# Attention with a top-1 mixture of experts: order of the weight loads, layout of the second weights, and columns of the first product in steps of two

## The chip, the cores and the metric

One core of a Trainium2 chip runs the whole program. The metric is device time in microseconds of one execution; three executions of the kernel before are listed, and one more was recorded with a profile. Engines are called PE (TensorE), PEld (its weight loads), DVE (VectorE), ACT (ScalarE), POOL (GpSimd) and SP (SyncE, which issues most transfers).

## The reference

Block-causal attention over 8 batches of 8 heads, 576 positions of 64 elements, then a mixture of experts over the 4608 tokens of 512 elements, all in float32:

```python
scores = q @ k.T / 8, masked to block_i >= block_j (blocks of 64), softmax, @ v
x = attention output as (4608, 512)
logits = x @ w_gate                       # (4608, 8)
expert = argmax(logits); gate = softmax(logits)[expert]
for e in range(8):
    tok = tokens of expert e, at most capacity (80) of them, those of largest gate
    h = relu(x[tok] @ w1[e])              # w1[e]: (512, 1024)
    out[tok] = gate[tok] * (h @ w2[e])    # w2[e]: (1024, 512)
all other rows of out are 0
```

Each of the sixteen weight matrices is 2 MiB.

## The kernel before, in words

**Attention.** 32 pairs of heads run as a software pipeline whose order is written out by hand: the loop at line 895 goes over turns `i`, and each turn issues the steps of a table (`FIRST`, `SHARED`, `TURN`, `LAST`) for the pairs around `i`. In a turn the pair `i+5` is loaded (`load`, line 613, 72 KB per transfer, read in runs of 128 bytes; SP issues most of them, POOL the second head's K from pair 5 on), the pair `i+2` is transposed on DVE (`prep`, line 639), the scores of pair `i+1` are made on PE (lines 663, 680, 689), and the probabilities of pair `i` are turned and multiplied with the values (lines 744, 770, 775, 776). Line 680 runs once per pair near a turn's start. The `ld` tiles have four buffers.

**Early weights.** The first three matrices of the list `w1[0], w2[0], w1[1], w2[1], ...` (`FW0 = 3`) are loaded during attention by POOL, in pieces of 128 rows (line 352: 512 KB for `w1`, 256 KB for `w2`), one piece in each turn with `i >= 2 and i % 3` (line 914).

**Selection.** After the last pair the tokens' gates are ranked (lines 978 to 1090), which ends with the row numbers `gi`. POOL then gathers the rows of experts 0, 1 and 2 (line 1101, `fetch`), 80 rows of 2080 bytes each; the other gathers follow one per expert.

**Later weights.** They are issued by SP in order (line 362, `piece`; each behind the one before on SP). Before the selection `half()` loads the first half of `w2[1]` (line 951). Its other half waits for the landing of the second gather (`HOLD = 1`, lines 1020 and 1199). The next loads wait, in turn, for the landing of the load or gather that stands in `behind` (lines 1200 to 1203):

```python
other_half(fetches[HOLD])
behind = [loaded.ins, fetches[HOLD]]
for _ in range(FWA + FWC + FWB - 1):
    weights(1, behind.pop(0))
    behind.append(loaded.ins)
```

so at most two are under way. From `w2[4]` on there is one `weights(1)` in the expert loop after the first product and one after the second (lines 1363 and 1372); those wait for a free buffer, of which there are nine.

**Experts.** For each expert PE makes the first product (`first`, line 1284, through `blocks`, line 1217: 128 pairs of a weight load of 64 columns of `w1` and a matmul over 80 tokens, at line 1240; the first half of expert 0 at line 1227), ACT applies the relu into `hT`, and PE makes the second product (`second`, line 1303, matmuls at line 1325 with `hT` as stationary and `w2` as moving operand). `divide` (line 1211, DVE) scales the gathered rows, `prepare` (line 1254) transposes them, and `scatter` (line 1340) writes the result rows. In expert 0 a check of the selection runs beside it (`finish_`): DVE makes `chk` at line 1162 and PE sums it at line 1166, between the two halves of the first product.

The rows of `w2` lie on the partitions as `(a p)`: row `128 a + p` on partition `p`, so each partition takes runs of 512 elements, 2 KB. `w1` lies in the same way with runs of 1024 elements, 4 KB.

Of the kernel before, what the change touches and what calls it, by code (L numbers as in the profile page):

```python
# [7 lines left out]
F32 = mybir.dt.float32  # L8
# [10 lines left out]
P = 128  # L19
# [169 lines left out]
def tile_attn_moe(ctx, tc, q, k, v, w_gate, w1, w2, capacity, out, xs=None, dbg=None):  # L189
    nc = tc.nc  # L190
# [152 lines left out]
    def loads(n, after=None):  # L343

        nonlocal nw, loaded
        for _ in range(n):
            src, e = wlist[nw]
            w_ = wpools[nw % len(wpools)].tile([P, KP * F], F32, name="w")
            nw += 1
            wt_[src is w2, e] = w_ = w_.rearrange("p (a f) -> p a f", f=src.shape[2])  # L350
            if nw <= FW0:
                yield from (nc.gpsimd.dma_start(w_[:, a], src[e][a * P:(a + 1) * P]) for a in range(w_.shape[1]))
                continue
            piece(w_, src[e], 0, w_.shape[1], after)

    def piece(w_, src, a0, a1, after=None):

        nonlocal loaded
        with ExitStack() as order:
            if loaded is not None:  # L360
                order.enter_context(tc.issue_after(loaded.ins))
            loaded = nc.sync.dma_start(w_[:, a0:a1], src[a0 * P:a1 * P].rearrange("(a p) f -> p a f", p=P))
        if after is not None:
            tc.add_manual_dep(loaded.ins, after.name, mybir.DependencyInfo(
                mybir.DependencyClass.Sync, mybir.DependencyReason.DATA))

    def half():

        nonlocal nw
        src, e = wlist[nw]  # L370
        w_ = wpools[nw % len(wpools)].tile([P, KP * F], F32, name="w")
        nw += 1
        wt_[src is w2, e] = w_ = w_.rearrange("p (a f) -> p a f", f=src.shape[2])
        na = w_.shape[1]
        piece(w_, src[e], 0, na // 2)
        return lambda after: piece(w_, src[e], na // 2, na, after)

    Pt = [{u: pb.tile([P, 2, w], F32, name=f"P{u}_{i}") for u, w in WIDE.items()} for i in range(2)]  # L380

# [510 lines left out]
    with tc.manual_schedule():  # L892
        warm(WARM[0], banks("g")[0])
        early = loads(FW0)
        for i in range(-LEAD, n):
            held.clear()
            if i == -1:
                nc.sync.dma_start(ci, capacity.bitcast(U32).partition_broadcast(P))
                for h in range(2):
                    nc.sync.dma_start(wgd[h * D:(h + 1) * D, :, h * E:(h + 1) * E], wg_v[h])  # L900

            for _ in range(min(5, nz - kept - cleared) if i >= n - 5 else 0):
                clear(cleared, nc.sync)
                cleared += 1
            if i == 1 - LEAD:
                nc.scalar.activation(early_exp, ramp[:, 2, 0:1], AF.Exp)
                constants()
            if i == -1:
                constants2()
            if i == 5:  # L910
                nc.gpsimd.tensor_copy(cf, ci)
            if i == 7:
                constants3()
            if i >= 2 and i % 3:
                next(early, None)
            shared = i > 1 and (i < NP or i % NP == 0)
            for d, what, *args in FIRST if i == -1 else AHEAD if i == -2 else LAST if i == n - 1 else SHARED if shared else TURN:
                if what in slots_:
                    slots_[what]()
                elif 0 <= i + d < n and not (what == "flip" and n - NP <= i + d < n - 2):  # L920
                    getattr(pairs[i + d], what)(*args)
            if n - NP <= i + valued < n - 2:
                pairs[i + valued].flip()
            if i >= flipped and (i - flipped) % NP == NP - 1 and i - flipped < n - 1:
                enqueue(batches[(i - flipped) // NP])
        for _ in early:
            pass
        while not turns:
            t()
        bt = batches[B - 1]  # L930
        pairs[n - 2].flip()
        for _ in recips[0]:
            pass
        bt.store_sums()
        pairs[n - 1].take("V00", "a")
        bt.flip(NP - 1, 0, 8)
        pairs[n - 1].take("V01", "a")
        pairs[n - 1].take("V1", "v")
        att.close()
        fwa = late.enter_context(tc.tile_pool(name="fwa", bufs=FWA, **right, **tw))  # L940
        wpools += [fwa] * FWA
        bt.logits2(LAST_BANKS)
        bt.logits_by_token(NP - 1)
        bt_, mark = turns.pop(0)
        bt_.turn2(banks("av")[0])
        mark()
        for _ in bt.products(range(NP - 1)):
            pass
        bt.flip(NP - 1, 8, S // 32)
        bt.store_x()  # L950
        other_half = half()
        for _ in (*bt.products((NP - 1,)), *bt.shift()):
            pass
        bt.expo()
        nc.gpsimd.tensor_copy(seen[0:1], dl[0:1, 0, 0:1])
        found, weighed = bt.first_of(), bt.weight()
        for g_ in (found, found, found, weighed, found, weighed):
            next(g_)
        bt.turn_gated()
        bt.turn2(banks("L")[0])  # L960
        while small:
            t()
        for _ in bt.placed():
            pass
# [52 lines left out]
        for h in range(2):  # L1017
            vec.max_index(cidx[:, h], cand16[:, h], Wf[:, h * HW:(h + 1) * HW])

    HOLD = 1  # L1020
    pen = sel.tile([P, 2, NH], F32, name="pen")
    pool.tensor_scalar(pen, key, scalar1=0.0, scalar2=8192.0, op0=ALU.is_lt, op1=ALU.mult)
    pool.tensor_tensor(pen, pen, iota_c[:, 0:NH].unsqueeze(1).broadcast_to([P, 2, NH]), op=ALU.add)
# [172 lines left out]
    wpools += [fwc] * FWC + [fwb] * FWB  # L1196

    assert cleared == nz or ov is None
    other_half(fetches[HOLD])
    behind = [loaded.ins, fetches[HOLD]]  # L1200
    for _ in range(FWA + FWC + FWB - 1):
        weights(1, behind.pop(0))
        behind.append(loaded.ins)

# [9 lines left out]

    def blocks(dst, w_, x_, n, nb, after=None, pieces=None):
        if pieces is not None:
            for a in range(n):
                pieces(a, after)  # L1220
                for b in range(nb):
                    for c in range(2):
                        col = (2 * b + c) * 64
                        with ExitStack() as order:
                            if after is not None:
                                order.enter_context(tc.issue_after(after.ins))
                            after = nc.tensor.matmul(dst(b)[64 * c:64 * (c + 1)], lhsT=w_[:, a, col:col + 64],
                                                     rhs=x_[a], start=(a == 0 and b == 0),
                                                     stop=(a == n - 1 and b == nb - 1))
                yield after  # L1230
            return
        for b in range(nb):
            for a in range(n):
                for c in range(2):
                    col = (2 * b + c) * 64
                    with ExitStack() as order:
                        if after is not None:
                            order.enter_context(tc.issue_after(after.ins))
                            after = None
                        last = nc.tensor.matmul(dst(b)[64 * c:64 * (c + 1)], lhsT=w_[:, a, col:col + 64],  # L1240
                                                rhs=x_[a], start=(a == 0), stop=(a == n - 1))
                    yield last

# [330 lines left out]
```

## Time and profile before

| | |
|---|---|
| three executions | 385.63, 386.33, 386.37 us, median 386.33 |
| profiled execution | 387.1 us, of which the span of its instructions is 385.3 |
| granted TensorE clock | 0.997 |
| PE, DVE, ACT, POOL busy | 367.5, 286.0, 287.5, 183.7 us |
| transferred | 84.43 MB, mean 219 GB/s |

Attention takes the first 276 us or so, the selection until about 288, the experts until 378.8, and the last scatter and the end of the program the rest. Stretches are read by busy time per engine; DMA share is the mean busy share of 16 transfer engines and can pass 1.

### The profile page before, as it was taken

The numbers are of one execution on the slowest core, as the hardware profiler recorded it, in microseconds if no ns is written. First come the engines' busy times: TensorE is split into PE (matmuls) and PEld (weight loads), VectorE is DVE, ScalarE is ACT, GpSimd is POOL, SyncE is SP. The second block draws the span as 40 slices with busy tenths as digits, with TensorE's granted clock in tenths as the row PEclk, the third lists the DMA queues.
The fourth block names the chain that finished last, engine by engine and source line by source line (L and its number), as shares of the span: only waits on it lengthen the run. The fifth ranks groups of instructions, "written<-read, shape, count | busy, mean of one in ns | idle before, by whom it ended". The sixth has DMA issues, their size and how long they took to land. (4 is left out here: it accounts for less than half of the span.)

```text
span 385.3 us, 15173 instructions
## 1 busy us (share of the span) xinstructions
PE 367.5 (95%) x5973; PEld 248.4 (64%) x5973; DVE 286.0 (74%) x804; ACT 287.5 (75%) x880; POOL 183.7 (48%) x377
## 2 busy tenths in 40 slices
PE   5899899999999999999999999999999999999983
PEld 3566567666766666676676676666668555555652
DVE  5889799999999999999999999999986210101001
ACT  1799799999999999999999999999521333332221
POOL 6246376665976766786587664430132121110000
PEclk9999999999999999999999999999999999999998
DMA  9969999999999999999999999999795899999950
GB/s 125 154 120 187 133 184 173 154 231 132 164 215 151 162 202 181 155 176 196 177 174 245 145 182 191 279 393 407 157 212 167 278 384 374 384 391 398 399 211 26
DMA packets 169937, 84.43 MB, mean 219 GB/s; under 512 B 132590, under 2 KB 151886, under 8 KB 169857
## 3 DMA queue, kind: packets, MB, share of 16 engines
q1 hardware_dynamic: 158368, 61.80, 76.3%
q0 software_dynamic: 9120, 21.27, 24.2%
q8 instruction: 49, 0.80, 1.0%
q10 hardware_dynamic: 2368, 0.30, 0.6%
q14 instruction: 32, 0.25, 0.3%
HBM read 63.21 MB, written 20.33 MB: 217 GB/s over the span
## 5 line engine op out<-in xcount | busy, mean ns | idle before, releaser
L710 ACT ACTIVATE P<-bank,negm 128x512 f32<-128x512 f32 (+3 forms) x320 | 157.6, 549 | 10.6 <-DVE negm L699 5.9
L663 PE MATMUL bank<-T,qt 64*128 64x320 f32 (+3 forms) x512 | 98.8, 494 | 1.4 <-DVE PT L792 1.3
L770 PE MATMUL bank<-PT,vn 128*64 128x64 f32 (+3 forms) x1288 | 88.9, 292 | 0.0
L699 DVE TENSOR_REDUCE negm<-bank 128x1 f32<-128x320 f32 (+2 forms) x192 | 83.4, 474 | 5.6 <-PE bank L689 5.4
L792 ACT COPY PT<-bank 128x512 f32<-128x512 f32 x149 | 77.2, 636 | 3.8 <-PE bank L744 3.3
L770 PEld LDWEIGHTS bank<-PT,vn 128*64 128x64 f32 x1288 | 57.1, 137 | 26.7 <-ACT PT L792 3.4
L646 POOL TENSOR_SCALAR qt<-T 128x128 f32<-128x128 f32 (+2 forms) x96 | 31.2, 344 | 88.4 <-DVE T L639 88.4
L744 PEld LDWEIGHTS bank<-ident,P 64*128 64x128 f32 (+1 forms) x1600 | 58.0, 137 | 11.8 <-issue 6.6
L663 PEld LDWEIGHTS bank<-T,qt 64*128 64x128 f32 x512 | 47.9, 187 | 26.8 <-ACT PT L792 15.2
L744 PE MATMUL bank<-ident,P 64*128 64x64 f32 (+1 forms) x1600 | 63.5, 225 | 1.3 <-ACT P L710 0.6
L710 ACT ACTIVATION_READ_ACCUMULATOR P<-bank,negm 128x1 f32 x256 | 61.7, 241 | 0.0
L699 DVE TENSOR_REDUCE raw<-bank 128x1 f32<-128x64 f32 (+1 forms) x128 | 51.8, 444 | 2.3 <-PE bank L663 2.0
L639 DVE STREAM_TRANSPOSE T<-ld 128x576 f32<-128x576 f32 x64 | 49.1, 768 | 5.7 <-DMA ld<-in_k_dram 4.0
L632 POOL DMA_DIRECT2D vn<-in_v_dram x58 | 45.8, 792 | 1.2 <-issue 0.7
L1325 PE MATMUL av<-w,hT 128*32 128x512 f32 (+2 forms) x320 | 39.0, 553 | 0.0
L624 POOL DMA_DIRECT2D ld<-in_k_dram x54 | 37.3, 695 | 2.7 <-DMA ld<-in_q_dram 2.7
L1334 DVE SCALAR_TENSOR_TENSOR y<-av,comb,yt 80x512 f32<-80x512 f32 (+1 forms) x8 | 5.6, 696 | 43.0 <-ACT yt L1332 42.9
L1240 PE MATMUL ps<-xsT,w 128*64 128x80 f32 x896 | 33.1, 234 | 0.3 <-issue 0.3
L1240 PEld LDWEIGHTS ps<-xsT,w 128*64 128x64 f32 x896 | 31.9, 137 | 1.9 <-PE av L1325 1.0
L1340 POOL DMA_INDIRECT out_dram<-y,si x8 | 7.5, 936 | 53.6 <-DVE y L1334 41.3
L1332 ACT ACTIVATE yt<-ps,gfar 32x512 f32<-32x512 f32 (+2 forms) x18 | 11.4, 635 | 26.1 <-PE ps L1325 26.0
L792 DVE COPY PT<-bank 128x512 f32<-128x512 f32 x43 | 29.3, 683 | 0.3
(202 smaller groups left out, 423.9 us busy)
## 6 DMA issues: line engine op xcount, KB each, us to landing
w<-in_moe_w_dram SPq DMA_DIRECT2D x12, 2048.0 KB, 17.6
xs<-Y SPq DMA_DIRECT2D x32, 288.0 KB, 5.5
out_dram<-zero SPq DMA_DIRECT2D x18, 512.0 KB, 7.6
ld<-in_q_dram SPq DMA_DIRECT2D x126, 72.0 KB, 5.5
vn<-in_v_dram POOLq DMA_DIRECT2D x58, 128.0 KB, 5.1
ld<-in_k_dram SPq DMA_DIRECT2D x72, 72.0 KB, 5.3
w<-in_moe_w_dram POOLq DMA_DIRECT2D x8, 512.0 KB, 6.6
ld<-in_k_dram POOLq DMA_DIRECT2D x54, 72.0 KB, 6.4
```

Of the source, the lines that this page charges most:

```text
L624: eng.dma_start(self.nat[x][r], (q, k)[x][b, h0 + h, :, 32 * i:32 * i + 32] .rearrange("(g r) d -> r g d", r=32))
L632: eng.dma_start(self.vn[:, h], v[b, h0 + h, 0:512].rearrange("(j p) d -> p j d", p=P))
L639: nc.vector.transpose(t, self.nat[x].rearrange("p g d -> p (g d)"))
L646: nc.gpsimd.tensor_scalar(qb[:, to], tb[:, of], scalar1=SCALE, scalar2=1.0, op0=ALU.mult, op1=ALU.mult)
L663: nc.tensor.matmul(s[h][:, c:c + n], lhsT=q_[:, P * t - BLK:P * t + BLK], rhs=k_[:, 0:n], start=(c == 0 and g != "2"), stop=(g == "1"))
L699: nc.vector.tensor_reduce(to[:, b, h:h + 1], self.s[g][h][:, c:c + n], axis=AX.X, op=ALU.max, negate=True)
L710: nc.scalar.activation(Pt[self.i % 2][u][:, h, c1:c1 + n], self.s[g][h][:, c:c + n], AF.Exp, bias=self.negm[:, t, h:h + 1], scale=1.0, acc ...
L744: nc.tensor.transpose(pt[c][0:cols.stop - cols.start, n_ * BLK:(n_ + 1) * BLK], row[u][r, h, cols], ident[r, r])
L770: nc.tensor.matmul(a4[r] if c0 is None else av[r, BLK * c0:BLK * (c0 + b1 - b0)], lhsT=self.vn[:, h, j, :], rhs=self.PT[:, h, row, b0:b1]. ...
L792: (nc.scalar.copy if (eng or TAKE[x]) == "a" else nc.vector.tensor_copy)(*self.out.pop(x))
L1240: last = nc.tensor.matmul(dst(b)[64 * c:64 * (c + 1)], lhsT=w_[:, a, col:col + 64], rhs=x_[a], start=(a == 0), stop=(a == n - 1))
L1325: last = nc.tensor.matmul(to[col:col + s1 - s0, c0:c1], lhsT=hT[:, a, s0:s1], rhs=w_[:, a, c0:c1], start=(a == ends[0]), stop=(a == ends[1 ...
```

## The change

The half load goes; `w2[1]` is loaded whole, and it and the next load both wait for the landing of the first gather. Early pieces go out in turns with `i >= 6 and i % 3`, and those of `w2[0]` are four of 512 KB. In every `w2` a partition gets two neighbouring rows per group of 256 (row `256 g + 2 p + j` on partition `p`), which is a run of 4 KB. So that the hidden units of `hT` lie in the same order, the first product's blocks take columns of `w1` in steps of two (`pairs_of`).

```diff
             if nw <= FW0:
+                if src is w2:
+                    to, of = in_twos(w_, src[e])
+                    yield from (nc.gpsimd.dma_start(to[:, g], of[:, g]) for g in range(to.shape[1]))
+                    continue
                 yield from (nc.gpsimd.dma_start(w_[:, a], src[e][a * P:(a + 1) * P]) for a in range(w_.shape[1]))
                 continue
-            piece(w_, src[e], 0, w_.shape[1], after)
+            load_w(w_, src is w2, src[e], after)
+
+    def in_twos(w_, src):
+        return w_.rearrange("p (g j) f -> p g (j f)", j=2), src.rearrange("(g p j) f -> p g (j f)", p=P, j=2)
...
-            loaded = nc.sync.dma_start(w_[:, a0:a1], src[a0 * P:a1 * P].rearrange("(a p) f -> p a f", p=P))
+            loaded = nc.sync.dma_start(*(in_twos(w_, src) if twos else (w_, src.rearrange("(a p) f -> p a f", p=P))))
...
-            if i >= 2 and i % 3:
+            if i >= 6 and i % 3:
                 next(early, None)
...
-        other_half = half()
...
-    HOLD = 1
+    HOLD = 0
...
-    other_half(fetches[HOLD])
-    behind = [loaded.ins, fetches[HOLD]]
-    for _ in range(FWA + FWC + FWB - 1):
+    behind = [fetches[HOLD], fetches[HOLD]]
+    for _ in range(FWA + FWC + FWB):
         weights(1, behind.pop(0))
         behind.append(loaded.ins)
...
+    def pairs_of(b, c):
+        at = 256 * (b // 2) + 128 * c + b % 2
+        return slice(at, at + 127, 2)
...
-                        col = (2 * b + c) * 64
+                        cols = pairs_of(b, c)
...
-                            after = nc.tensor.matmul(dst(b)[64 * c:64 * (c + 1)], lhsT=w_[:, a, col:col + 64],
+                            after = nc.tensor.matmul(dst(b)[64 * c:64 * (c + 1)], lhsT=w_[:, a, cols],
...
-                        last = nc.tensor.matmul(dst(b)[64 * c:64 * (c + 1)], lhsT=w_[:, a, col:col + 64],
+                        last = nc.tensor.matmul(dst(b)[64 * c:64 * (c + 1)], lhsT=w_[:, a, cols],
```

## Rows read from the trace of the kernel before

**Rows 1.** The page: busy time, share and instructions; PE's busy tenths in 40 slices.

```profile
PE 367.5 (95%) x5973; PEld 248.4 (64%) x5973; DVE 286.0 (74%) x804; ACT 287.5 (75%) x880; POOL 183.7 (48%) x377
...
PE   5899899999999999999999999999999999999983
```

**Rows 2.** Stretches of attention: busy us (x instructions) per engine, clock, DMA share, GB/s.

```profile
32.00:42.00 10.00, 9.81 (x159) 7.09 (x159) 7.03 (x17) 8.92 (x27) 6.50 (x12) 1.00 1.19 188
50.00:60.00 10.00, 10.00 (x182) 6.93 (x179) 9.71 (x26) 9.62 (x30) 7.35 (x14) 1.00 1.21 185
180.00:230.00 50.00, 50.00 (x851) 34.48 (x848) 48.42 (x127) 49.11 (x159) 34.68 (x71) 1.00 1.14 184
250.00:270.00 20.00, 19.96 (x341) 13.72 (x335) 18.49 (x52) 19.02 (x61) 4.11 (x9) 1.00 1.03 398
```

**Rows 3.** Timeline of PE, line 680: start us, us, what, once per pair.

```profile
22.32 0.30 PE L680 MATMUL bank<-T,qt 64*64 64x64 f32 x8
...
30.09 0.33 PE L680 MATMUL bank<-T,qt 64*64 64x64 f32 x8
...
39.13 0.24 PE L680 MATMUL bank<-T,qt 64*64 64x64 f32 x1
...
48.19 0.43 PE L680 MATMUL bank<-T,qt 64*64 64x64 f32 x8
...
56.05 0.30 PE L680 MATMUL bank<-T,qt 64*64 64x64 f32 x8
```

**Rows 4.** Timelines of DVE and PE around 42 us, idle time before in brackets.

```profile
41.42 0.78 DVE L639 STREAM_TRANSPOSE T<-ld 128x576 f32<-128x576 f32 x1 [2.78 <-DMA ld<-in_k_dram]
...
43.36 1.99 PE L663 MATMUL bank<-T,qt 64*128 64x512 f32 x12 [1.28 <-DVE PT L792]
```

**Rows 5.** Timelines of POOL and SP: early pieces, and a K load.

```profile
31.95 0.59 POOL L352 DMA_DIRECT2D w<-in_moe_w_dram  x1
...
58.18 0.59 POOL L352 DMA_DIRECT2D w<-in_moe_w_dram  x1
...
32.05 1.09 SPq L624 DMA_DIRECT2D ld<-in_k_dram  x2
```

**Rows 6.** Stretches of the expert stage, columns as in rows 2.

```profile
299.00:301.00 2.00, 2.00 (x21) 0.60 (x24) 0.00 (x0) 0.44 (x1) 0.96 (x1) 1.00 0.32 31
301.00:371.40 70.40, 70.05 (x1240) 43.07 (x1233) 10.31 (x33) 22.56 (x40) 10.46 (x11) 1.00 1.03 383
```

**Rows 7.** Timeline of PE: the last expert's first product and the start of its second.

```profile
367.00 4.65 PE L1240 MATMUL ps<-xsT,w 128*64 128x80 f32 x128
373.38 0.52 PE L1325 MATMUL pm<-w,hT 128*32 128x384 f32 x3 [1.73 <-SPq L1386]
```

**Rows 8.** Timeline of SP: the first weight loads behind the gathers.

```profile
293.28 0.39 SPq L362 DMA_DIRECT2D w<-in_moe_w_dram  x1
...
299.33 0.92 SPq L362 DMA_DIRECT2D w<-in_moe_w_dram  x2
```

**Rows 9.** Timelines of DVE, PE and POOL at the first expert; the gathers' median landing.

```profile
291.94 0.29 DVE L1211 TENSOR_TENSOR xn<-xg 80x128 f32<-80x128 f32 x1 [0.50 <-DMA xg<-xs,gi]
...
296.71 2.29 PE L1240 MATMUL ps<-x,w 128*64 128x80 f32 x60
...
291.43 0.97 POOL L1101 DMA_INDIRECT xg<-xs,gi  x1 [0.31 <-issue]
...
295.05 0.27 DVE L1211 TENSOR_TENSOR xn<-xg 80x128 f32<-80x128 f32 x1
...
xg<-xs,gi POOLq DMA_INDIRECT x8, 6.8
...
296.61 0.17 PE L1166 MATMUL pm<-chk,ones 128*128 128x10 bf16 x1
```

**Rows 10.** Groups by line and form: busy us, mean ns of one, idle before.

```profile
L1240 PEld LDWEIGHTS ps<-xsT,w 128*64 128x64 f32 x896 | 31.9, 137 | 1.9 <-PE av L1325 1.0 <-issue 0.4
L663 PEld LDWEIGHTS bank<-T,qt 64*128 64x128 f32 x512 | 47.9, 187 | 26.8 <-ACT PT L792 15.2 <-issue 5.1 <-DVE PT L792 1.8
...
L1240 PE MATMUL ps<-xsT,w 128*64 128x80 f32 x896 | 33.1, 234 | 0.3 <-issue 0.3
```

More of the change, by code (lines that the diff above doesn't have):

```diff
@@ L351, in loads, with load_w @@
             if nw <= FW0:
+                if src is w2:
+                    to, of = in_twos(w_, src[e])
+                    yield from (nc.gpsimd.dma_start(to[:, g], of[:, g]) for g in range(to.shape[1]))
+                    continue
                 yield from (nc.gpsimd.dma_start(w_[:, a], src[e][a * P:(a + 1) * P]) for a in range(w_.shape[1]))
                 continue
-            piece(w_, src[e], 0, w_.shape[1], after)
-    def piece(w_, src, a0, a1, after=None):
+            load_w(w_, src is w2, src[e], after)
+    def in_twos(w_, src):
+        return w_.rearrange("p (g j) f -> p g (j f)", j=2), src.rearrange("(g p j) f -> p g (j f)", p=P, j=2)
+    def load_w(w_, twos, src, after=None):
         nonlocal loaded
@@ L365, in piece @@
                 mybir.DependencyClass.Sync, mybir.DependencyReason.DATA))
[L367 to L376, printed above, removed]
     Pt = [{u: pb.tile([P, 2, w], F32, name=f"P{u}_{i}") for u, w in WIDE.items()} for i in range(2)]
@@ L1234, in blocks @@
                 for c in range(2):
-                    col = (2 * b + c) * 64
+                    cols = pairs_of(b, c)
                     with ExitStack() as order:
```

## The prediction

> **What bounds the kernel now.** I read the page first, then stretches, then single waits. PE is busy for 95% of the span [rows 1], so only a few microseconds can be won, where PE stands still. The busy tenths show where: besides the first slices and the selection, slice 5 (38.5 to 48 us) has an 8, and the end falls off [rows 1].
>
> At the first place, 32 to 42 us, DVE is busy 7.03 of 10 us and the DMA share is 1.19; later, as in 180 to 230 us, PE runs without a gap [rows 2]. The starts of line 680, one per pair of heads, give the beat: 7.77 us (22.32 to 30.09), then 9.04 and 9.06 (to 39.13 and 48.19), then 7.86 [rows 3]. Two turns are too long by 1.2 each against their neighbours, 2.5 us together. What they wait for: DVE stands 2.78 us for the K tile of a later pair, after which PE idles 1.28 us [rows 4]. Just ahead are the first early piece of the weights, issued by POOL at 31.95, and the K loads of that pair, which SP issues only at 32.05 [rows 5] and which land at 41.4, 9.4 us later.
>
> At the second place, the expert stage, DMA and PE run level. From 301 to 371.4 us PE is busy for 70.05 of 70.4 us and DMA moves 383 GB/s at a share of 1.03 [rows 6]. But the last first product ends at 367.00 + 4.65 = 371.65 and the last second product begins at 373.38, after 1.73 us of idle that is put to SP, that is to the last weights [rows 7]; their data had ended at about 371.4, 2.0 us before. So the weights are late by less than two microseconds, at the very end. The lateness was made at the start: SP waits until 293.28, loads a half, and issues the next loads only at 299.33, when that has landed [rows 8]. In 299 to 301 us DMA moves 31 GB/s [rows 6].
>
> **The change part by part.**
>
> *Early pieces from turn 6.* The three pieces up to 58.18 us [rows 5] go away there; twelve of 512 KB come at the places of turns 7 to 23, in place of sixteen. POOL saves four issues of 0.59 us [rows 5]; it is busy 48% [rows 1], so that is 0. Of the three, the latter two cost nothing now (PE is busy 10.00 of 10 us between 50 and 60 [rows 2]). The first is 0.524 MB. At 398 GB/s, which DMA reaches in another stretch [rows 2], it holds the engines for 1.3 us, where they are never free [rows 2]. What is queued behind it, the K tile above all, can land 1.3 us earlier. Lower bound 0 (the K tile is late through SP's own backlog); upper bound the whole excess of 2.5. I take 1.3, since the K tile's queue shortens by just that. Turns 13 to 17 get 512 KB where 256 KB stood; pieces of 512 KB go out between 180 and 230 us too, with PE at 50.00 of 50 [rows 2], so 0; should that cover go, 1.3 per piece at worst.
>
> *No half load, weights behind the first gather.* The half lay under the selection and nothing waited for it; the gathers wait for the selection's indices and not for it, so its removal gains nothing there, and 1.05 MB more must come later. In return SP starts when the first gather lands, about 291.9 (DVE begins on it at 291.94 [rows 9]), with two whole loads at once. Data follow an issue by about 1.7 us (299.33 [rows 8], full rate from 301 [rows 6]), so they move from 293.6 on. Loads go in order with two outstanding: the third is issued when the first has landed, while the second still moves, so I see no gap. The sum: 70.4 us at 383 GB/s are 26.96 MB, of which 25.17 are twelve loads. After the change it is 26.96 + 2.10 (the load of `w2[1]`) + 0.17 (the third gather) = 29.2 MB, 76.3 us at the same rate; from 293.6 that ends at 369.9 instead of 371.4, 1.5 us earlier. With the same 2.0 us from the end of data to PE the second product starts at 371.9, and 0.25 of the idle 1.73 stays. Buffers don't hold this up: the first to be taken again, that of `w1[0]`, is read for the last time by the first product that begins at 296.71 [rows 9]. Bounds: 0, and 1.73, where PE becomes the limit.
>
> *Two rows per partition in `w2`.* The same bytes in runs of 4 KB, like those of `w1`, in place of 2 KB. The 383 GB/s [rows 6] are a mean over both; the stretch in which the output is cleared, mostly by 4 KB runs, gives 398 [rows 2], 4% more with other traffic in it. Half the bytes at 4% would be 1.5 us, but the cap of 1.73 leaves 0.25 of it. I take 0 and keep that for the range.
>
> *Columns in steps of two.* 1024 pairs of weight load and matmul keep their count. No row shows TensorE loading weights in steps. Below: 0, since a gain is excluded where as many elements are read from further apart. Above: as if the whole span of 128 columns were read, by the nearest rows: a load of 64 columns takes 137 ns, one of 128 columns 187 (L663) [rows 10]. The loads fill 31.9 of the 33.1 us of 896 pairs [rows 10], so there is no cover, and 36% more on 1024 pairs (37.8 us) is 13.8 us. I take 0: the columns loaded are still 64, so the row of 64 is the nearest.
> The Trainium skill speaks to this ("SBUF — State Buffer", section "Door 1: The DMA port swizzle"): SBUF is read in lines of 16 bytes, each crossing to another line has a price, and two hits per line are enough to hide it. Four-byte elements in steps of two still hit each line twice, so the sum by that rule would be 0 too, at its very edge; no run here shows it.
>
> Sum: 1.3 + 1.5 = 2.8 us. The profiled execution took 387.1 us with a span of 385.3, 0.8 over the median of 386.33. The differences carry over: span 382.5, own time 384.3, median **383.5**.
>
> **Rivals.** *A. Only the tail gains.* K stays late because SP issues it at 32.05 with a backlog, whatever POOL does: 386.3 - 1.5 = 384.8. For it: 9.4 us from issue to landing. Against it: the DMA share of 1.19 [rows 2], which says the engines and not SP are short.
> *B. The gathers pay.* Two whole loads now start while the third gather moves. Issued at 291.43, it now lands before 295.05, within 3.6 us, since DVE goes on with it there unhindered; the median of all eight is 6.8 [rows 9]. At 6.8 it lands at 298.2. Behind it on DVE stands a count whose result comes 1.1 us later and feeds the matmul of 296.61, which stands in PE's queue ahead of the first product's second half [rows 9]. PE then waits 2.7 us; less the 1.73 of idle at the end that this absorbs, the tail loses 1.0, and with 1.3 from the start-up the time is 386.0. It decides from a landing later than 295.5. Against it: the gather's issue ends at 292.4, the weights' data come at 293.6.
> *C. Slower: strided weight loads.* TensorE pays for the steps as bounded above: +13.8. The lateness of DMA goes whole (-1.73), the start-up gives -1.3: 386.3 + 10.8 = 397.1. It decides as soon as a pair becomes longer by 3 us / 1024, some 3 ns of its 37. For it: the loads' busy share in that stage. Against it: nothing measured.
> *D. It doesn't do what it says.* Each load still waits for the last but one; if gaps remain between them as now, the tail gains little and the result lies at 385.0.
>
> **How the numbers follow.** Forecast 0.60, A 0.12, D 0.04, B 0.11, C 0.13. Two tenths of a per cent, 0.77 us, is about what a measurement of this kernel can tell from no change. Forecast, A, D and a hundredth of B are faster, 0.77; the rest of B is within 0.2%, 0.10; C is slower, 0.13. The range leaves C out and holds the rest: from 386.3 - 2.5 - 1.73 = 382.1 to B's 386.0.
>
> **What would show it.** Right: the turns of 9.04 and 9.06 lose 1.3 between them and DVE's wait of 2.78 for K shortens; DMA moves about 380 GB/s from 294 on without the hole at 299; the wait of 1.73 ahead of the last second product falls under 0.5; a load of 64 columns still takes 137 ns and a first product 4.65 us. Wrong: that load longer (C), DVE waiting for `xg` at 295 (B), the K wait as long as before (A).

## The result and the profile after

| | before | after |
|---|---|---|
| median of six executions, same chip | 386.87 us (385.63 to 388.76) | 382.29 us (381.79 to 385.53) |
| ratio after / before | | 0.9888, 95% interval [0.9845, 0.9932] |
| profiled execution, its span | 387.1, 385.3 us | 382.09, 380.4 us |

The change makes the kernel 1.1% faster, 4.6 us by the medians; 382.29 lies in the predicted range and 1.2 us under the predicted 383.5. Ratios, here and below, leave out executions that took over 1.5% more than the fastest of the same kernel; medians keep them. The two profiled spans differ by 4.9 us. The last pair's row of line 680 (line 674 in the changed kernel) starts at 258.29 us instead of 260.73, so attention and its start-up gave 2.44 us. From the first `xn` to the last expert's second product it takes 79.00 us (289.50 to 368.50) instead of 81.44 (291.94 [rows 9] to 373.38 [rows 7]), so the experts gave 2.44 too.

From the page of the changed kernel: busy time, and PE's busy tenths in 40 slices.

```profile
PE 366.7 (96%) x5973; PEld 247.5 (65%) x5973; DVE 285.9 (75%) x804; ACT 286.9 (75%) x880; POOL 181.0 (48%) x373
...
PE   5899999999999999999999999999999999999993
```

Against [rows 1], PE's work is the same to a microsecond; the 8 in the slice behind 38 us and the 8 ahead of the last slice are gone.

Stretches of the changed kernel, columns as in [rows 2]: the start-up, attention twice, its end, and the experts.

```profile
32.00:42.00 10.00, 10.00 (x163) 7.01 (x159) 9.12 (x21) 9.41 (x29) 5.82 (x11) 1.00 1.09 166
50.00:60.00 10.00, 10.00 (x156) 6.59 (x156) 9.81 (x25) 9.61 (x31) 4.60 (x9) 1.00 1.20 153
180.00:230.00 50.00, 49.95 (x831) 34.33 (x832) 48.61 (x127) 49.09 (x157) 32.35 (x66) 1.00 1.13 177
...
310.00:360.00 50.00, 50.00 (x892) 30.71 (x888) 7.23 (x21) 16.71 (x30) 7.64 (x8) 1.00 1.03 395
...
364.00:366.00 2.00, 2.00 (x60) 2.00 (x62) 0.75 (x1) 0.68 (x1) 0.20 (x1) 1.00 0.59 233
...
366.00:367.00 1.00, 1.00 (x36) 1.00 (x32) 0.00 (x0) 0.44 (x1) 0.71 (x1) 1.00 0.12 49
```

Between 32 and 42 us DVE is busy 9.12 us where it was 7.03 [rows 2]. From 310 to 360 us PE has no gap, and the last two lines show the sides exchanged: the transfers run out from 364 us on, and in the trace the last packet of weights ends at 367.0, 1.5 us before the last second product begins (368.50), so PE and no longer the weights sets the end. In the kernel before that packet ends at 372.7, 0.7 us before PE goes on.

PE's timeline in the changed kernel: the pair starts that answer to [rows 3], then the last first product and the start of its second, which answer to [rows 7].

```profile
22.24 0.30 PE L674 MATMUL bank<-T,qt 64*64 64x64 f32 x8
...
29.99 0.32 PE L674 MATMUL bank<-T,qt 64*64 64x64 f32 x8
...
38.57 0.30 PE L674 MATMUL bank<-T,qt 64*64 64x64 f32 x8
...
46.09 0.32 PE L674 MATMUL bank<-T,qt 64*64 64x64 f32 x8
...
53.84 0.30 PE L674 MATMUL bank<-T,qt 64*64 64x64 f32 x8
...
363.92 4.65 PE L1236 MATMUL ps<-xsT,w 128*64 128x80 f32 x128
368.50 0.52 PE L1321 MATMUL pm<-w,hT 128*32 128x384 f32 x3
```

The turns of 9.04 and 9.06 became 8.58 and 7.52. The second product follows its first product with no idle time in brackets, where 1.73 us stood.

DVE's and SP's timelines in the changed kernel: the K tile that was waited for in [rows 4], and the weight loads of [rows 8].

```profile
38.46 0.73 DVE L633 STREAM_TRANSPOSE T<-ld 128x576 f32<-128x576 f32 x1
```

```profile
289.66 9.68 SPq L369 DMA_DIRECT2D w<-in_moe_w_dram  x3
```

The K tile is there when DVE comes for it. SP's first loads go out 0.16 us after DVE begins on the first gather's rows (289.50), as the change says.

Groups by line and form in the changed kernel, against [rows 10]:

```profile
L1236 PE MATMUL ps<-xsT,w 128*64 128x80 f32 x896 | 32.6, 233 | 0.0
L1236 PEld LDWEIGHTS ps<-xsT,w 128*64 128x64 f32 x896 | 31.4, 138 | 1.4 <-issue 0.9
```

A load of 64 columns in steps of two takes 138 ns, side by side it took 137.

### The profile page after: what moved, and what is told of

The parts are those of the page before. It is cut to its first block, busy times and chain, and to the rows that moved or that the text cites. A ratio compares the mean times of both kernels' runs of the same rounds, so it can differ in the third digit from the quotient of the medians.

```text
span 380.4 us, 15167 instructions
## 1 busy us (share of the span) xinstructions
PE 366.7 (96%) x5973; PEld 247.5 (65%) x5973; DVE 285.9 (75%) x804; ACT 286.9 (75%) x880; POOL 181.0 (48%) x373
## 4 chain that ended last, share of the span: by engine, by line
PE 85%; DVE 8%; ACT 3%; DMA 2%; issue 1%; POOL 0%; POOLq 0%; ACTq 0%; SPq 0%; DVEq 0%
PE bank L764 21%; PE bank L657 20%; PE bank L738 13%; PE av L1321 9%; PE ps L1236 9%; PE bank L432 2%; PE bank L769 2%; DMA ld<-in_q_dram 2%; ACT P L704 2%; DVE raw L693 2%; DVE negm L693 1%; PE ps L796 1%; PE bank L674 1%; PE pm L1321 1%; DVE T L633 1%; PE bank L446 1%
## 5 line engine op out<-in xcount | busy, mean ns | idle before, releaser
L1321 PE MATMUL av<-w,hT 128*32 128x512 f32 (+3 forms) x320 | 39.3, 554 | 0.0
L1328 ACT ACTIVATE yt<-ps,gfar 32x512 f32<-32x512 f32 (+2 forms) x18 | 11.4, 634 | 24.5 <-PE ps L1321 24.4
```

The lines of the kernel that those rows point to most:

```text
L1321: last = nc.tensor.matmul(to[col:col + s1 - s0, c0:c1], lhsT=hT[:, a, s0:s1], rhs=w_[:, a, c0:c1], start=(a == ends[0]), stop=(a == ends[1 ...
```

## The experiments

Twelve kernels, on two chips, each compared with the kernel before on its own chip. There the kernel before spreads widely (384.9 to 391.7 us in 33 executions beside the first four kernels), so ratios carry intervals of 0.3 to 0.6% to each side, and variants that differ by less than that aren't told apart by time. What tells them apart is two lengths read from each profile, one profile per row of the table. **Three turns**: from the row of line 680 that starts at 30.09 us in [rows 3] to the one at 56.05 (25.96 us), where the first early piece falls. **Seven rounds**: from the start of expert 0's second product to that of expert 7's, which leaves out the selection.

| kernel | early pieces from turn | order behind gathers | `w2` runs | ratio to before [95%] | three turns | seven rounds |
|---|---|---|---|---|---|---|
| before | 2 | old | 2 KB | 1 | 25.96 | 74.45 |
| changed, the result above | 6 | new | 4 KB | 0.9888 [0.9845, 0.9932] | 23.85 | 72.01 |
| changed, again | 6 | new | 4 KB | 0.9891 [0.984, 0.9941] | 23.26 | 72.37 |
| e1 | 2 | new | 4 KB | 0.9986 [0.9939, 1.0032] | 24.33 | 71.77 |
| e5 | one at 2, rest from 6 | new | 4 KB | 0.9913 [0.9879, 0.9947] | 24.23 | 73.44 |
| e4 | 6 | old | 2 KB | 0.9905 [0.9876, 0.9935] | 23.38 | 75.11 |
| e7 | 2 | new | 2 KB | 0.9942 [0.9909, 0.9975] | 24.98 | 73.21 |
| e2 | 6 | new | 2 KB | 0.9931 [0.9895, 0.9967] | 23.23 | 73.31 |
| e3 | 6 | old | 4 KB | 0.9939 [0.9904, 0.9975] | 23.24 | 71.67 |
| e12 | 6 | old | 4 KB | 0.9881 [0.9832, 0.993] | 23.26 | 71.89 |
| e13 | 6 | old | 4 KB | 0.9881 [0.9839, 0.9923] | 23.23 | 71.90 |
| e14 | 6 | new | 4 KB | 0.9874 [0.9831, 0.9917] | 23.25 | 72.33 |
| e10 | 6, every other turn | new | 4 KB | 0.9896 [0.9841, 0.9951] | 23.68 | 71.93 |
| e9 | 6 | new | 8 KB | 1.0627 [1.0565, 1.069] | 23.25 | 94.46 |

A third quantity is the **lead** of a tile in attention: from the end of SP's last issue of a pair's K or Q loads to DVE's transposition of that tile, worked out for every pair from the two timelines. The smaller it is, the nearer DVE is to waiting.

### The change again, on another chip

> The changed kernel itself, for times beside the others on one chip. Here the kernel before ranged from 384.9 to 391.7 us in the runs of the first four experiments, while the one with early pieces from turn 6 alone stayed within 383.1 to 385.1. Theory 2 (the early pieces eat the loads' lead over their use; where it runs out, PE stands and the time is some us longer in part of the executions): the changed kernel, whose lead falls to about 7 us where the twelve pieces come in 17 turns, lies at 381.8 to 382.5 in most executions, with a few up to 387. Rival (the spread of times belongs to the chip and hits every kernel alike): its times spread as those of the kernel before, over 6 us.

Measured: median 383.37 us (381.92 to 384.67), ratio 0.9891, as in the result above; one execution of six lies in the expected 381.8 to 382.5, and the spread is half of that of the kernel before beside it (385.01 to 390.34, in 23 executions). Its profile (span 382.9) has the short start-up, and three turns later in attention that the first profile doesn't have: 8.75 for 7.78 (with a gap of PE put to "issue"), and later 9.25 and 8.79 for 8.69 and 8.28. The lead explains the latter two: at pair 27 it is down to 4.0 us for K and 4.4 for Q, and DVE waits 1.11 us for Q:

```profile
224.96 0.78 DVE L633 STREAM_TRANSPOSE T<-ld 128x576 f32<-128x576 f32 x1 [1.11 <-DMA ld<-in_q_dram]
```

In the first profile the lead is 8.8 and 7.1 there. The last pair's row comes at 260.37 us in this second profile, 258.29 in the first, 260.73 in the kernel before. So the changed kernel, too, runs close to the edge of its transfers in attention.

### Early pieces from turn 2 again

```diff
-            if i >= 6 and i % 3:
+            if i >= 2 and i % 3:
```

> The changed kernel with the early pieces from turn 2 again (twelve pieces of 512 KB, the first three in turns 2, 4 and 5); all else as changed. Theory 1 (the piece of turn 2 made the K tile late): the turns of 9.04 and 9.06 us of the kernel before come back, DVE waits 2 to 3 us for K near 40 us, and the span is 2.4 us longer than the changed kernel's 380.4, so 382.8. Rival (the start-up gain came from the transfers' layout or from chance): the turns stay at 8.6 and 7.5 and the span within 0.5 us of 380.4.

Measured: 389.61 us (384.4 to 393.01), ratio 0.9986. Nearly the whole gain of the change is gone, but, in this profile, not where the prediction had put it: the three turns cost 24.33 us, only 0.5 to 1.1 more than in the changed kernel. DVE's timeline and stretches of this kernel, later in attention:

```profile
157.98 0.78 DVE L633 STREAM_TRANSPOSE T<-ld 128x576 f32<-128x576 f32 x1 [0.87 <-DMA ld<-in_k_dram]
...
163.83 0.78 DVE L633 STREAM_TRANSPOSE T<-ld 128x576 f32<-128x576 f32 x1 [3.45 <-DMA ld<-in_q_dram]
```

```profile
162.00:164.00 2.00, 0.00 (x0) 0.00 (x0) 0.17 (x1) 0.33 (x3) 0.00 (x0) 1.00 0.63 97
164.00:166.00 2.00, 0.67 (x8) 0.48 (x8) 2.00 (x6) 0.64 (x3) 1.23 (x4) 0.79 0.75 122
166.00:168.00 2.00, 2.00 (x20) 1.28 (x19) 1.35 (x6) 1.88 (x8) 2.00 (x4) 0.50 0.91 168
168.00:170.00 2.00, 2.00 (x32) 1.59 (x30) 1.01 (x2) 0.30 (x1) 1.91 (x4) 0.50 1.23 176
170.00:172.00 2.00, 2.00 (x30) 1.73 (x28) 1.65 (x4) 1.79 (x4) 1.49 (x4) 0.51 1.41 149
172.00:174.00 2.00, 2.00 (x32) 1.59 (x30) 1.36 (x4) 1.68 (x5) 0.00 (x0) 1.00 1.19 122
```

Q is late by 3.45 us, PE stands for 3.66, and from then until 172 us the granted clock is 0.50 (1.2 instead of 2.4 GHz). The two turns take 12.54 and 11.36 us, where the same two turns of the changed kernel take 8.69 and 8.34: 6.9 us for two tiles that were late by 0.87 and 3.45. The lead tells why here: it peaks at 17 us, falls as piece follows piece, and is 5.0 for Q at pair 15 and 6.9 at pair 19, the one that is late (3.45 of the 6.9 are DVE's wait); the changed kernel has 11.3 and 12.3 there. This is one profile; that the wide spread of the kernel before comes from such stalls too is likely, and not shown.

### One piece at turn 2, the rest from turn 6

```diff
-            if i >= 6 and i % 3:
+            if (i == 2 or i >= 6) and i % 3:
```

> The changed kernel with the first early piece in turn 2, the other eleven from turn 7 on as in the change. Theory 1 (that one piece costs the start-up 2.4 us): line 680's counterpart takes about 18 us for the two turns after 30 us, against 16.1 in the changed kernel, and the profile is 1.9 us longer. Theory 2 (the piece takes its own transfer time, 1.3 us or somewhat more, from a lead of 3 to 7 us, and how much of it PE feels differs from run to run): the two turns take between 16.1 and 17.5 us, and the lead of the pairs after the tenth is as in the changed kernel or better, since one piece less comes later.

Measured: 384.03 us, ratio 0.9913, beside 0.9891 for the changed kernel: not told apart. The three turns take 24.23 us, so a single piece of 512 KB at turn 2 costs about 1.0 us against the 23.2 to 23.3 of most profiles without it; two turns take 16.4 us (30.53 to 46.90), not the 18 of theory 1. Its seven rounds are 1.1 to 1.4 us longer than the changed kernel's; a row of PE at the first second product shows where (the idle time is put to "issue", to none of the waits):

```profile
298.92 0.62 PE L1321 MATMUL ps<-w,hT 128*32 128x512 f32 x1 [0.78 <-issue]
```

### The kernel before with its pieces from turn 6

```diff
-            if i >= 2 and i % 3:
+            if i >= 6 and i % 3:
```

> The kernel before with the early pieces from turn 6 and nothing else changed (sixteen pieces as before, the last in turn 29). Theory 1 (start-up and tail add up): the span is 2.4 us shorter than 385.3, 382.9, with the wait for K near 40 us gone and the tail's idle of 1.7 us ahead of the last second product as before. Rival (the tail hides it): within 0.5 us of 385.3.

Measured: 384.31 us (383.12 to 385.1), ratio 0.9905. This line alone carries most of what the whole change does to the median, and it has the narrowest spread of all with ten or more executions. Its three turns take 23.38 us. Its leads stay at 14 us or more from pair 8 on and end over 20; eight of its sixteen pieces are of 256 KB. The experts are as in the kernel before, with weights late at the end:

```profile
371.10 0.52 PE L1325 MATMUL pm<-w,hT 128*32 128x384 f32 x3 [1.78 <-SPq L1386]
```

### The kernel before with the new order alone

```diff
-        other_half = half()
...
-    HOLD = 1
+    HOLD = 0
...
-    other_half(fetches[HOLD])
-    behind = [loaded.ins, fetches[HOLD]]
-    for _ in range(FWA + FWC + FWB - 1):
+    behind = [fetches[HOLD], fetches[HOLD]]
+    for _ in range(FWA + FWC + FWB):
```

> The kernel before with the order of the later weights alone: no half load, w2[1] whole and the next load both behind the first gather; early pieces from turn 2, single rows and columns side by side as before. Theory 1 (the order starts the stream earlier and the tail gains what it can): no hole in the transfers near 299 us, the last weights' data 1.5 us earlier relative to the first gather, the wait ahead of the last second product 0.3 us or less instead of 1.7, and the stretch from the first gather's landing to the last second product 79.7 us or less instead of 81.4. Rival (without the longer runs the rate is too low, and the 1 MB more eats the earlier start): the wait stays above 1 us.

Measured: 385.07 us, ratio 0.9942. The seven rounds fall from 74.45 to 73.21 us: 1.24, near the 1.5 that the prediction gave to the order. The last round takes 10.02 us where it took 11.81, so the wait for the last weights is nearly gone, as expected; but a gap of 1.10 us has come at the first second product, and with it the stretch from the first gathered rows to the last second product is 80.3 us instead of the expected 79.7 or less.

### The changed kernel without the layout

Single rows of `w2` again, in the same pieces, and columns side by side.

```diff
-                    to, of = in_twos(w_, src[e])
-                    yield from (nc.gpsimd.dma_start(to[:, g], of[:, g]) for g in range(to.shape[1]))
+                    to, of = w_, src[e].rearrange("(a p) f -> p a f", p=P)
+                    yield from (nc.gpsimd.dma_start(to[:, 2 * g:2 * g + 2], of[:, 2 * g:2 * g + 2]) for g in range(4))
...
-            loaded = nc.sync.dma_start(*(in_twos(w_, src) if twos else (w_, src.rearrange("(a p) f -> p a f", p=P))))
+            loaded = nc.sync.dma_start(w_, src.rearrange("(a p) f -> p a f", p=P))
...
-        at = 256 * (b // 2) + 128 * c + b % 2
-        return slice(at, at + 127, 2)
+        at = 64 * (2 * b + c)
+        return slice(at, at + 64)
```

> The changed kernel with one row per partition in w2 (runs of 2 KB) and the first product's columns side by side again; order of loads and early pieces as changed. Theory 1 (the longer runs of w2 raised the rate of the expert stage from 383 to 396 GB/s): the rate falls back to 383 to 385 from 292 to 364 us, the data end about 2.4 us later, near 368, PE waits 1 us or less ahead of the last second product, and the span is 0 to 1 us longer. Rival (the rate rose because loads no longer drained in the first microseconds or for some other reason): the rate stays at 394 or more and the span within 0.3 us of 380.4. If steps of two slow TensorE's weight loads, a first product gets shorter than 4.65 us; I expect 4.65.

Measured: 384.58 us, ratio 0.9931. Seven rounds take 73.31 us, 1.6 over the 71.67 in which PE makes them unhindered (the next experiment). Of that 1.31 us is a gap at the first second product and 0.28 a wait for the last weights; the rows of PE (the first stands at the end of the gap, its bracket gives a part of it):

```profile
298.07 0.62 PE L1321 MATMUL ps<-w,hT 128*32 128x512 f32 x1 [0.72 <-issue]
...
369.61 0.52 PE L1321 MATMUL pm<-w,hT 128*32 128x384 f32 x3 [0.28 <-SPq L1382]
```

And the rate of the transfers in the middle of the experts, to be read against 395 GB/s in the same stretch of the changed kernel (first the kernel before, then e2):

```profile
310.00:360.00 50.00, 49.73 (x855) 29.78 (x848) 7.23 (x21) 15.97 (x29) 8.28 (x9) 1.00 1.04 387
...
310.00:360.00 50.00, 50.00 (x892) 30.80 (x888) 7.24 (x21) 16.71 (x30) 7.59 (x8) 1.00 1.04 387
```

### The changed kernel with the old order

The half load under the selection and `HOLD = 1` are back, in the new layout (the half is two of the four groups).

```diff
...
+        other_half = half()
...
-    HOLD = 0
+    HOLD = 1
...
-    behind = [fetches[HOLD], fetches[HOLD]]
-    for _ in range(FWA + FWC + FWB):
+    other_half(fetches[HOLD])
+    behind = [loaded.ins, fetches[HOLD]]
+    for _ in range(FWA + FWC + FWB - 1):
```

> The changed kernel with the half load ahead of the selection and its other half behind the second gather, the other loads as in the kernel before; layout and early pieces as changed. Theory 1 (the order starts the stream of weights earlier, and that is most of the tail's gain): the hole of two microseconds after the second half comes back near 297 us, the data end 1 to 2 us later than the 365.5 of the changed kernel, and since they ended 2.5 us before PE wanted them the span is 0 to 0.5 us longer. Rival (the order is the whole gain of the tail): PE waits about 1.7 us ahead of the last second product and the span is 382 or more.

Measured: 385.04 us, ratio 0.9939, its interval overlapping the changed kernel's. The profile, of its fastest execution: the hole of the transfers is back (78 GB/s from 296 to 300 us), and yet seven rounds take 71.67 us, the shortest of all, with no wait at the end, though the loads are issued in the old order. The stretch of the experts:

```profile
310.00:360.00 50.00, 50.00 (x892) 30.80 (x888) 7.22 (x21) 16.71 (x30) 7.64 (x8) 1.00 1.03 397
```

So the rate comes with the layout, not with the order, and by the rounds the layout makes PE the limit without the order. The times don't show a gain from it: e4, with the same early start and order but without the layout, has 384.31 us and 0.9905.

### Pieces of 256 KB, with either order

The four early pieces of `w2[0]` become eight of 256 KB, so that sixteen pieces go out in turns 7 to 29, in both kernels; the first of them (e12) has the old order as in the diff above, the second (e14) is the changed kernel otherwise. In these pieces a partition's runs are 2 KB again. A third (e13) is the first with POOL instead of SP issuing the values of pair 2.

```diff
-                    yield from (nc.gpsimd.dma_start(to[:, g], of[:, g]) for g in range(to.shape[1]))
+                    yield from (nc.gpsimd.dma_start(to[:, g, 512 * j:512 * (j + 1)], of[:, g, 512 * j:512 * (j + 1)]) for g in range(to.shape[1]) for j in range(2))
```

> The changed kernel with the old order of the later weights (half load, other half behind the second gather) and the early w2 in eight pieces of 256 KB, so sixteen pieces from turn 7 to 29; rows and columns as changed. Theory 4 (with the longer runs the rate is enough for the tail without the new order; the new order puts 0.3 to 1.4 us on TensorE at the first second product, where its code arrives late behind the weights): the first two second products start 10.3 us apart, the stretch from the first gathered rows to the last second product is 78.8 us, and the times lie at 381.2 to 382.5 with no slow ones, since the lead of the loads stays above 14 us from the eighth pair on. Rival (the new order is needed): PE waits 1 us or more ahead of the last second product.

> The changed kernel with the early w2 in eight pieces of 256 KB, sixteen pieces from turn 7 to 29; the order of the later weights as changed. Theory 2: the lead stays above 14 us in the middle, the slow executions vanish. Theory 4: the first two second products start 10.4 to 11.8 us apart and the time is 0.3 to 1.4 us longer than its sister with the old order. Rival: no difference between the two orders.

> As the kernel with the old order and sixteen pieces, and the third pair's values are issued by POOL instead of SP. Theory (what is left of the start-up excess, 0.4 to 0.8 us in the third turn, is the wait for these values behind SP's backlog): the turn after 30 us takes 7.8 us, the time is 0.3 to 0.8 us shorter than its sister. Rival (POOL's issues in the start-up delay the K loads that it issues): the same or longer.

Measured: 383.33, 382.05 and 382.86 us; ratios 0.9881, 0.9874 and 0.9881. None can be told from the changed kernel (0.9888 and 0.9891); e14 has the lowest median, and nothing more is claimed for it. The expected 0.3 to 1.4 us between the two orders is not there, and of the expectation that no long executions are left, only e14 bears it out (381.78 to 384.05): e12 has five from 381.4 to 384.0 and two of 389.8 and 390.0. The leads fall under the expected 14 us, to 8.2 in e12 and 11.0 in e14. e12 differs from e3 by the size of these pieces alone; 0.9881 and 0.9939 lie 0.6% apart with intervals that overlap, so that smaller pieces help is possible, and not shown. Against e4 (0.9905) it differs by the layout alone, and that gain isn't shown by the times either. Their attention is clean in all three profiles: 235.1 to 235.3 us from the third pair's row (22.24 us in the changed kernel) to the last one's, against 236.05 and 237.61 in the two profiles of the changed kernel. Moving the values of pair 2 gains nothing: its turn is 7.83 us with it and 7.85 without. In e12, whose profiled execution is one of its longest (span 388.0), the selection waits for the stores of attention's output; POOL's row at the first gather:

```profile
290.36 1.14 POOL L1117 DMA_INDIRECT xg<-xs,gi  x1 [7.97 <-DMA xs<-Y]
```

There the first gather starts 32.5 us after the last pair's row, 27.96 in the changed kernel.

### A piece every other turn

```diff
-            if i >= 6 and i % 3:
+            if i >= 6 and i % 2:
```

> The changed kernel with its twelve early pieces in every other turn from 7 to 29 instead of two turns in three from 7 to 23. Theory 2: the lead of K and Q over their use stays at 12 us or more from the eighth pair to the end, the slowest executions vanish, and the times stay within 381.5 to 383.0, the median the same as the changed kernel's best or up to 1 us under its median. Rival (the lead has nothing to do with the spread): times and spread as the changed kernel's.

Measured: 383.65 us (382.05 to 385.95, expected 381.5 to 383.0), ratio 0.9896; in the profile (span 384.2) the leads are larger than in the changed kernel from pair 14 to pair 26, as they should be, though 9.7 us at the least and not 12, and fewer pieces per turn gain nothing in time. The first gather starts 30.4 us after the last pair's row instead of 27.96, with a granted clock of 0.990 over the whole. Whether that is due to the last pieces, which now fall at 235 and 252 us, is open: that lag is 30.2 us in e13, but 28.7 in e14 and 28.0 in e4, all three with pieces up to turn 29. The nine profiles with the last piece out by turn 25 have 27.95 to 27.98 us, so late pieces are the likely cause, and not shown to be.

### Four rows per partition, columns in steps of four

```diff
-        return w_.rearrange("p (g j) f -> p g (j f)", j=2), src.rearrange("(g p j) f -> p g (j f)", p=P, j=2)
+        return w_.rearrange("p (g j) f -> p g (j f)", j=4), src.rearrange("(g p j) f -> p g (j f)", p=P, j=4)
...
-        at = 256 * (b // 2) + 128 * c + b % 2
-        return slice(at, at + 127, 2)
+        at = 256 * c + b
+        return slice(at, at + 253, 4)
```

> The changed kernel with four rows per partition in w2 (runs of 8 KB) and the first product's columns in steps of four. Theory 3 (TensorE reads a stationary operand in steps of two at no cost because two elements still share a line of its memory, and a wider step costs): a load of 64 columns gets longer than 137 ns, a first product longer than 4.65 us. Rival (the step doesn't matter to a load of four-byte elements at all): 137 ns and 4.65 us as before. For the transfers: if the rate follows the length of the run, the weights move above the 397 GB/s of runs of 4 KB, by less than the 3% that 2 to 4 KB gave.

The early pieces of `w2[0]` are two of 1 MB by this edit, so ten pieces go out in turns 7 to 20.

Measured: 410.99 us, ratio 1.0627. The group of the loads, and one first product:

```profile
L1236 PEld LDWEIGHTS ps<-xsT,w 128*64 128x64 f32 x896 | 54.3, 216 | 1.4 <-issue 0.9
```

```profile
320.48 7.91 PE L1236 MATMUL ps<-xsT,w 128*64 128x80 f32 x128
```

A load of 64 columns takes 216 ns instead of 138, a first product 7.91 us instead of 4.65. Eight products with 3.26 us more each are 26.1 us; the profiled span is 27.2 longer than the changed kernel's. Rival C exists, then, but one step further: a step of two is free, a step of four costs more than rival C's bound of 187 ns. What longer runs give beyond 4 KB stays open. The same stretch as above:

```profile
310.00:360.00 50.00, 50.00 (x666) 34.59 (x667) 4.96 (x16) 11.76 (x22) 6.75 (x7) 1.00 1.02 404
```

That is 404 GB/s against 395 to 397, and a packet of 8 KB moves 25.5 bytes per ns in it, one of 4 KB in the changed kernel 24.5, as the expectation had it. From 292 to 368 us, though, the two means are alike, 24.5 and 24.4.

## Why the prediction was right, and where its terms were off

**The time.** Forecast 383.5 us with 382.1 to 386.0; measured 382.29. Both places named were the right ones, and each gave more than was said (2.44 for 1.3, 2.44 for 1.5). That the time lies in the range is in part luck: the range allows a gain of 4.23 us at most, the medians differ by 4.58 and the profiled spans by 4.9, and it fits because the kernel before has a median of 386.87 in six executions where the forecast started from 386.33 in three. The 0.2% that the prediction thought a measurement can tell was too small; the interval here is 0.4% to each side.

**Early pieces, 1.3 us.** The mechanism was right: without a piece at turn 2 the wait of 2.78 us for K is gone, and the three turns are shorter in every profile without one. The size in these two profiles, 2.11 of the 2.44 us, is one draw from a spread. The three turns with a piece there take 25.96, 24.98, 24.33 and 24.23 us (before, e7, e1, e5; mean 24.88); the ten without 23.23 to 23.85 (mean 23.36). The difference of the means is 1.5 us, near the 1.3 worked out from the piece's bytes; that the kernel before was read in a costly execution is likely, and not shown. That the latter two pieces cost nothing was read from windows with PE at 10.00 of 10 us, and that reading was too narrow. PE doesn't stand in them, but a piece there eats lead that the loads need later: with all pieces from turn 2 in e1, PE stood not at turn 2 but at 162 us. The larger pieces of turns 13 to 17, also taken at 0, aren't free in the profiles either: from the third pair's row to the last one's, the four kernels with pieces from turn 6 and 256 KB there (e4, e12, e13, e14) take 235.1 to 235.4 us, the four profiles with 512 KB (changed twice, e2, e3) 235.8 to 237.6. By e4, which moves the pieces and nothing else, the move is worth 0.95% [0.65, 1.24], or 3.7 us of 388.46 on that chip, more than twice the term and most of the whole gain.

**Order of the loads, 1.5 us.** By itself it did what was worked out: 1.24 us in e7 (74.45 to 73.21 us), or 1.8 from e4 to e2 (75.11 to 73.31), and of the wait 0.28 stayed in e2 where 0.25 was forecast. Its gap at the first second product, 1.1 to 1.3 us, was not foreseen. But the changed kernel didn't need this term to lose the 1.73 us, since e3 has the old order and no wait. The 2.0 us between the last data and PE were misread: the last packet of weights ends at 372.7, 0.7 before PE goes on; this lag is the same on both sides of the sum and drops out.

**Two rows per partition, 0: the step that failed.** The prediction saw that runs of 4 KB might give 1.5 us by the 398 GB/s of another stretch, and took 0 because the order's 1.5 left only 0.25 to gain. It should have been the first term. In 310 to 360 us all kernels of 2 KB runs that were read move 387 or 388 GB/s (before, e2, e7, e4), and those of 4 KB 395 and 397 (changed, e3); from 292 to 368 us the mean packet is 90 ns for 2 KB in the kernel before and 168 for 4 KB in the changed one, so two short ones take 13 ns more than one long. Read as a table of seven rounds:

```
                  2 KB runs               4 KB runs
old order   74.45 (before), 75.11 (e4)   71.67 (e3), 71.89 (e12), 71.90 (e13)
new order   73.21 (e7), 73.31 (e2)       72.01, 72.37 (changed), 71.77 (e1), 71.93 (e10), 72.33 (e14), 73.44 (e5)
```

With the layout and the old order the rounds are within 0.23 us of PE's own pace (six of 10.30 and a last one of 9.87 are 71.67); with the new order on top of it they are 0.1 to 0.7 over it, in e5 1.8. The two terms are not to be summed: either one nearly removes the wait, and the layout does it without the order's price. This rests on one profile of each kernel, in which e5 alone lets the layouts overlap; the times (e3 and e12 beside e4) are too wide to show it.

**The cap of 1.73 us** was low. The rounds of the kernel before are 10.42, 10.41, 10.29, 10.32, 10.87, 10.32 and 11.81 us; against 10.30 (six times) and 9.87 they lose 2.78 in all, 1.94 in the last and 0.57 in the fifth. The fifth shows no wait for weights; its row puts the gap to "issue" (the last section comes back to it):

```profile
350.97 0.36 PE L1240 MATMUL ps<-xsT,w 128*64 128x80 f32 x3 [0.27 <-issue]
```

The changed kernel's are 10.67, then 10.3 five times, and 9.87. So 2.78 went and 0.37 came, in the first round.

**Steps of two, 0.** Right: 138 ns for 137, first product 4.65 us. The rule of the Trainium skill that was cited ("SBUF — State Buffer", section "Door 1: The DMA port swizzle") has been put to the test by e9, and the traces agree: with lines of 16 bytes a step of two elements of four bytes hits each line twice and is free, a step of four hits it once and adds 78 ns per load; that the lines are the reason is the Trainium skill's account, the runs show the prices. That page of the Trainium skill also names four such elements as what one can stride for free; here the step of four is the one that costs, and the measurement decides.

**The rivals.** A (K stays late) fell: the wait is gone. B (the gathers pay) was half right: the third gather's rows are taken up 5.74 us after the first's, 3.11 before. But DVE has the count ahead of them in the changed program and doesn't wait for them, and the count's matmul comes 4.65 us after the first `xn`, 4.67 before; the prediction took DVE's order of the kernel before, so B failed for a reason that it had not weighed. C fell for a step of two. D fell too: no slice of 1.9 us from 292 to 364 us is under 326 GB/s, where [rows 6] had 31. **What none of them named** is the gap at the first second product: 1.31, 1.37 and 1.10 us in e2, e5 and e7, 0.5 in e14, some 0.3 in the changed kernel, 0.1 in e1, none in e9 and e10, where PE comes there later; no kernel with the old order has it.

## What to carry to other kernels

When two terms end the same wait, work out each as if the other weren't there, and see what the cheaper one leaves: here, by the profiles, the layout alone was enough. In a pipeline whose transfers are near saturation, count how far ahead the loads run, pair by pair, and not whether PE stands in the turn where a transfer is added: the bill comes many turns later, and in one profile here the engine that stood also lost its clock. A step of two four-byte elements in TensorE's stationary operand buys runs twice as long for the transfers at no price; a step of four does not.

## What the runs showed that was not expected

**Program code seems to share the way with the weights.** In the trace a packet of 16 KB of kind "instruction" starts 3.27 us after the first `xn` in the kernel before, and 2.57 to 4.7 in the other kernels with the old order. With the new order, where two whole loads of weights are ahead of it, it starts at 5.06 to 6.30. The three latest of all (5.99 in e7, 6.18 in e2, 6.30 in e5) are the three kernels in which PE has its gap of 1.1 to 1.4 us, about 7.5 us after the first `xn`, put to "issue". The times fit closer than that: in all seven profiles with a gap at this place (changed twice, e1, e2, e5, e7, e14) PE goes on 2.4 to 2.6 us after the packet's start, and in the seven without one PE comes there 3.3 us or more after it. The other gaps of over 0.4 us behind 30 us that are put to "issue" (c_after, e1, e3 and e9 near 139 us, e4 at 348.35) end 2.3 to 3.3 us after the start of such a packet, and so does the one in the fifth round of the kernel before (packet at 348.54, PE at 350.97). That PE waits for this code is inferred from these times; no run took a packet away.

**A stall can cost nearly twice its length.** In e1 PE stood for 3.66 us and the two turns became 6.9 longer, as the granted clock was at half (0.50) from 166 until 172 us.
